# Experts' outputs turned by DMA instead of TensorE, kv's columns permuted, and a new order of tasks

## The chip, the cores and the metric

The kernel runs on one NeuronCore of a Trainium2 chip. The metric is the device time of one execution in microseconds. The kernel before took 221.65 us (median of three runs, 221.53 to 222.14).

## What is computed

There are 8 batches of 576 tokens. A linear attention with 8 heads of 64 feeds a small mixture of 4 attention experts of which each token uses 2:

```
kv  = einsum('bhsd,bhse->bhde', k, v)              # per batch and head: 64 x 64
x   = einsum('bhsd,bhde->bhse', q, kv)
x   = x / sqrt(mean(x*x, -1) + 1e-6) * g_norm      # then heads side by side: (8, 576, 512)
w   = softmax over the best 2 of x @ w_gate        # 4 experts
for e in range(4):
    q, k, v = x @ wq[e], x @ wk[e], x @ wv[e]      # 64 wide
    a  = softmax(causal(q @ k.T / 8))
    out += w[e] * (a @ v @ wo[e])                  # 512 wide
```

## The kernel before

Everything is unrolled. The work is cut into tasks, each a name with a batch and one or two indices; a task is one engine's work on one tile. The string `ORDER` lists all tasks in the order in which they are issued, `ENGINE` says which of DVE (V), ACT (A) and POOL (G) takes each, and `SLOTS` which buffer each tile gets. A planner made the strings offline from costs and due times; each engine, and each DMA queue, works off its own tasks in that order. `ZEROS` puts products on zeros (matmuls that change nothing) ahead of some tasks, so that TensorE stays busy while it waits. SyncE (SP) issues nearly all DMAs in the order of the plan; one that waits holds back those behind it.

Tokens come in five blocks, four of 128 and one of 64. For each batch:

- `lk`, `lv`, `lq` load k, v and q (lines 309, 314, 321, 345); batches 0 and 1 (`NINE`) use another layout, and their q is turned by TensorE, while the later batches' q is turned on DVE (line 476).
- `kv` forms kv on TensorE; `kvc` copies it (line 283, where all copies out of PSUM are recorded) into `kvx`, which also holds, per head, four columns that make the gate's logits; `kgm` and `kgr` (lines 448, 455) compute these columns.
- `out` multiplies q by `kvx`. `oc` copies the result to `o_sb`; `sq`, `red`, `ln`, `rs` and `na` to `nc` make rstd; `xm` (line 562) multiplies x by rstd and sorts the 512 columns into four groups of every fourth column; `x` turns the groups on TensorE and `xc` copies them to `xT`.
- `gl`, `lg` and `m8` to `gate` make the gate's weights.
- `v`, `qp` and `kp` project x. Experts are taken in two pairs. `sc` makes the scores in four pieces, `exp` their exponentials (line 688), `msk` the causal mask (line 694), `pv` the product with v, in two groups of blocks.
- `rc`, `iv` and `oc2` (lines 725, 729, 736) scale the product by the gate over the softmax's sum into `osc`, 128 tokens x 5 blocks x 128 columns in bf16 for a pair.
- `ot` (line 277) turns the five blocks of `osc` on TensorE into PSUM, and `otc` (line 283) copies them to `OT`, of which there are two, for even and odd batches. In the last batch, both are in two parts.
- `y` multiplies `OT` by wo, `yc` copies the result, and `st` (line 779) stores it by SP.

All of TensorE's products are recorded at line 274, its transposes at line 277, all copies at line 283: groups are told apart by their tiles.

In `kvx` a pair of heads lies as four gate columns, 128 columns of kv, four gate columns. rstd's product reads x in order and writes every element to a place 128 elements from the last one:

```
out=short("x", b, i, dtype=FP32R)[:].rearrange("p (c m k r) -> p m k r c", c=NCH, m=NCH, k=2),
in0=ob[:, i, :, E : E + 2 * Dh].rearrange("p m (k r c) -> p m k r c", k=2, c=NCH),
```

Of the kernel before, what the change touches and what calls it, by code (L numbers as in the profile page):

```python
# [23 lines left out]
    ('q', 0, 1): 10, ('kv', 0, 0): 2, ('kv', 0, 1): 3, ('out', 0, 0): 8, ('out', 0, 3): 8,  # L24
    ('q', 1, 1): 8, ('kv', 2, 3): 8, ('out', 1, 4): 6,
# [3 lines left out]
    "04050c0e0100030d020S06070f090A2+0T0U0V320B0Y0I0a0Z0C0b0W0X0g0E2z2-0k5F310h5H0w0x0o0l080m0p305G0s0n0M0y0z1I0q1J"  # L29
    "130r181K333C34140i0G5L0j0t0u19150D165U0v7i1D0+1L0-1E5I0K5M1A1M1b1B1F3E353A101G361C1c3D3B387h5K1H1711371V3F393W"  # L30
    "5T3G5JAC127f3O1d7p0H5O1P1N7g1Q0J1Y3H1Z3P1O3I1S1R1a0N5S1T1W5R5P1U5W3X5V3K3J1X5N3S5Q3Q1e3L3TA47n3U5X3R1w1y3M3N0Q"
    "3Y0F1x3V3Z3a3bA6A31z2M2N2K27247j280L3c2L3d1o1q5Y5a1f1u1m1h257q7o2R1p211g1r5Z2U1v7u2S3e3t7s7r1n7t3h1i5d3f222V2O"
    "7w2P5c7vA51+2X3q2T3i1-3r5b3n3k2W5f3u3j7x262Y2Q5e3s5o5k3v5p5l5w5x3o29205q3l1s3m5m3p1j2Z1t1k3g5n5y2a4A4B4C4D1l5g"
    "5s5t5r4e237y5h7+5i3w7k5j2B2A4c7m4f5u5z2c7l0O4E4d2b5v5+5-3x2C2D3z602F612E0R4F422f43AFAHAG2G622g2H2d3y4P2e4Q4m2h"
    "4n4M2i636H687zCT82AI7-AJ2jAKAL4N4J4j6B4p4K4qAB4R6E696I4k6J654G832I48ADAE4O6A6UA944808188644H3+6V8C452JAO894I8A"
    "6K6L844r8D8E6F66490P2n3-6G6N2o6785CU2tCW462q40A7A8AA86CV47Ce6CEu2r6D2u6Y8K8B8LCb8M87AS8NEtCa8G6W6M8HAP6c4L4o6e"
    "6fAM8FCc7273Cd8I6O8J6dEw8O8P6Z6X704S4T6p416q716j8Q8R4g4hCgCiCf4U774X8S2w4V6k4Y4Z788e4WATCZCh4l4iAN6g6h6P2x748b"
    "6S75AR8c6T6l8Y8T8V2k4a6i8hCX8d6mAQAY6nCY2lCjCkCl4bAZAcAd79AkE-7D7ECoAeAl7A7BAa8Z8f8W6Q6a6b6oCm8X8i4s2vEv8gAb4t"
    "F18a4uAgAmAU8sAh4x4v6R8j9SF2HHAfAVCp908tAn6rAW7FAX4yAi9T7C914zAj4w92Ao939Q8U6s9RCt766tAp9d6x6uAq9eAr8k94959AF3"
    "6v9fF66wAs9BF49X9Y6y6zA-4+4-Cn7HAv7G8u7I7J6+59B29D8v5A7L7M5CAyCqF58+CrB5EzExCs7KF06-5D9E2sAwAtAx537NHICuF7CyF8"  # L40
    "547OCzAzE+Cv50B08l51CwF98wEy2yHKC+C-A+FAB18-8xBGBH7P9C96B6CxB7B3B4D4D8D0D5D997D6BqD1Br98FBAuD79ZDADBD2BsBtD3BQ"
    "BRFC7QDC7RBSB8BK8n7TBLDD8mBTDE7ZHJDF7UBdBe9a5E9bBU7aDGBV8y8o99B9BA7W8z9FDH9UFDBBFGHSDIBXBY8p8qDJ7XHVBZHU9V8rBO"
    "FH9HBP5552HM9GB+B-C1C2HTHW9WBCFFFE7cDY7d9IBuBvDMBaHYBW9cHXHZDb9J9KDNDOBbFM9L9MFNFODVDK56FY57FI9NHLHOBxDPDSDLHa"
    "DQFZDRFPBc9hByFJFKHNDWDXBDBMBNC0FaBIBJ9O9PFL9lDTDU9g9i9jFQ9mFRFUHbFV9nFbHRHcFWDs9k5BBEHeDk2pFXDtFSEE9oFTBwEFFc"
    "DZBzFdBf9pBgDaBFEGHfFeFfHPBhBiFgBlDqDlHQDiBmDmBjHdBnFhFmEHBkDrERE1ESDuE2DvDjDc9qHhHgDxFjFsD+9rFiHiFvDyDdFnDnDg"
    "BoBpD-HjDoDzETFpC3HmDpDhHyHnHoFoEOEIHzC5E3Hk9zEJFyDe9+EPC9HpF-FkFlC4FtFqFr9wFwFzC6H+DfFuC7EL9xCACBHqC8Hu7YHlEQ"
    "GAFxE07VH-HvEMHrF+HsDwG6CCGBCDGgGhHwE4E6HtG7HxI09sI1E7E8EKGeI2GGE5CECKGfGEI3I4GH9yE9GoEAI5IGCLCF7bGFEBCQGpA0A1"
    "CMGOGPGlCRG0I6GiGjI7ECI8G1IDG4IH9tI9IEED9uCS7SGmIMCNIAIBG5ENIJIIIFCOGRGSINGTGI2mGJGLEUG2EVEZIKCH9-GKGqICG8EWGM"
    "CIILIeIOEXCGGCGk9vG3EYEaEbG9IgIhEcIPIaIfGDGrIbGsIo587eCJIpEdGtIQGnIlImIiIUEnGvIVGNGuGQGwEoIcGxGyIjIdJ4J5GUGzGV"
    "J6J7GZGWEhG+IWEiA2EpIRG-GXGaCPInEjH0H1GbGYGcIqIkJHJIIrIsISIXJ8EqItGdHEHFHGJ9JAITJEJFJGErJBJCEsJJHBIYH5H6HCHDEk"  # L50
    "IZEeIuElEmJDJKEfIwIxJMJLH8H9IvIyJPJNJ0JOH7JQJRJ1JSH2JTJUEgIzH3JcHAJdH4I+JZI-J2JVJWJ3JeJaJbJfJgJiJXJYJjJhJk"
)
ENGINE = (
    "VVVVVVVVVVVVVVVGVGVVVGVVVVVAVVVAVVVVVAVVVAVAAVVAAVVVAVVAAVVVAVAAVGVAAVGVAAVGVAAVGVAAVVVVVVVAGVAGVAVVVGVVVGAVGV"
    "VGVVVAVAVAVAVAVVVAGVAGVAGVAGVVVVVVGVVAVAVAVAGVAGVAGVAGVVVVVVVVVVVVVVAVVAVVAVVVVVVVVVVVVAGVVVVAVAVAVAAVVAGVVVGV"
    "VAAVVVAVAAVVVVVVVAGVAGVVGVVGVVVGAVVVVVVAVAVVVVVAVAVAVAGVAGVAGVAGVVVVVVGVVVVAVAVAGVAGVAGVAGVVVGVVGVVVVVVVVVVAVV"
    "AVVAVVVVVVVVVVVVVVVVVVVVVVVVVVVVVAAVVVGVVAAVVVAVVVGVAAVGVGVGVAGVVGVAGVAGVAVGAVGVVGVVVVVAVAVAVVVAVAGVAGVAGVAGVV"
    "VGVVGVVAVVVAVAGVAGVAGVAGVVVGVVGVVAVAVVAVVVVVVVVVVVVVVVVVVVVVVVVVVVVAGVGVVVVVVVGVVAGVVAAVVAGVVAAVAAVGVGVGVAGVAG"
    "VAGVVGVVVVAVGVVVVVVVVAVVVAVAVVVAGVAGVAGVAGVVVVVVGVVAVAVAVAGVAGVAGVAGVVVGVVGVVAVVVVVVVAVVAVVVVVVVVVVVVVVVVVVVVV"
    "VVGVGVVVVVVAAVVVAVVAAVVAGVVVAVAAVGVGVGVAGVVGVAGVAGVAVGAVGVVVVAVVVVVAVAVVVAVAGVAGVAGVAGVVVGVVGVVVVAVVVAGVAGVAGV"  # L60
    "AGVVVVVVVVVAVVVVAVVAVVVVVVVVVVVVVVVVVVVVVVVVVAGVVVVVVVVAGVVVAVVVGVVAAVVAGVAAVGVGVGVVGVAGVVGVAGVVVGAVGVVGVAVVVA"
    "VAVAVAVAVAGVAGVAGVAGVVVGVVGVVVVAVAVAGVAGVAGVAGVVVVVVVVVVVAVVAVVVVVAVVVVVVVVVVVVVVVVVVVVVVVVVVVVVVVVAAVVVAVVAAV"
    "VAGVVVGVAAVGVGVGVVGVVGVAGVVVVVVGAVGVVGVAVAVVVAVVVVVAVAGVAGVAGVAGVVVVVVVVVVVAVVVAGVAGVAGVAGVVVGVVGVVAVAVVAVVAVV"
    "VVVVVVVVVVVVVVVVVVVVVVVAGVGVVVVVVAGVVAAVVAAVVVGVVVAVAAVGVGVGVVGVAVVAGVAGVVVGAVGVVGVVVVVVVAVVVVVAVAGVAGVAGVAGVV"
    "VVVVGVVAVAVVVAVAGVAGVAGVAGVVVGVVVVVVVVVVVVVVVAVVAVVVV"
)
SLOTS = (
    "00112326041501223046172011523620072123130483261500194A1513120B071320123854530148730301456A97021670211103018430"
    "0C101001113200B90313A27015145013140465547232417C5057143081103102202003043A2B3090013132B03328101456610207126020"
    "3201510322138321300103C3419160030321036744856721032210024835427032032005439A3143022400321202320923613302673043"  # L70
    "11620617201201761030201721506127456C013202303452303C120236200131452310C250450301165476723C4A521031004672261117"
    "00213045102413202167420320323112203264074190C10520617450091454427C1"
# [7 lines left out]
def names(nb):  # L80
# [3 lines left out]
    for b in range(nb):  # L84
# [7 lines left out]
        out += [("kvc", b, g) for g in range(1 + (b == 0))] + [(m, b, n) for n in r2 for m in ("kgm", "kgr")]  # L92
# [9 lines left out]
        for p in r2:  # L102
            out += [(m, b, p) for m in ("qp", "qpc", "kp", "kpc")]
            out += [(m, b, p, j) for j in r4 for m in ("sc", "exp", "msk")]
            out += [("pv", b, p, g) for g in r2] + [(m, b, p, g) for g in r2 for m in ("rc", "iv", "oc2")]
            out += [(m, b, p) + t for t in (((),) if b < nb - 1 else ((0,), (1,))) for m in ("ot", "otc")]
# [14 lines left out]
def kernel(  # L121
# [70 lines left out]
    ob = const.tile([P, NB, NCH, 2 * GW], FP32, name="o_sb")  # L192
# [18 lines left out]
    for j in range(2):  # L211
        kvx.append(const.tile([P, EP, 2 * GW], FP32, name=f"kvx{j}"))
        rstds.append(const.tile([P, NB * H], FP32, name=f"rstd{j}"))
        roots.append(const.tile([P, NB * H], FP32, name=f"root{j}"))
        t = const.tile([P, NB, H], FP32, name=f"ms{j}")
        nc.vector.memset(t[REM:P, NB - 1], 1.0)
        mss.append(t)
# [12 lines left out]
    for j in range(2):  # L230
        t = const.tile([P, NCH * S + PAD], FP32R, name=f"xT{j}")
        nc.vector.tensor_copy(out=t[:, NCH * S :], in_=zeros[:, 0:PAD])
        xTs.append(t)
        OTs.append(const.tile([P, EP * S], BF16, name=f"OT{j}"))
# [32 lines left out]

    def gates_of(t):
        return t[:].rearrange("p m (k g) -> p m k g", g=E)[:, :, :: 2 * GW // E - 1, :]
# [100 lines left out]
    def wg(m):  # L370
        rd_(nc.vector.tensor_tensor(
            out=wg_t[:, :, 2 * m : 2 * m + 2, :],
            in0=bank(m, "gb").rearrange("p (c d e) -> p e c d", c=2, e=E),
            in1=g_wide[:].unsqueeze(1).unsqueeze(2).to_broadcast([P, E, 2, Dh]), op=AluOpType.mult,
        ))
# [25 lines left out]
    def p_kv(b, n):  # L401
        if b in NINE:
            return big("kv", b, n if b == 0 else 0)[:, :, 0 : EP * Dh].rearrange("p a (m d) -> p m a d", m=EP)
# [34 lines left out]
    def of_part(b, g):  # L438
        return slice(g, g + 1) if b == 0 else slice(0, EP)

    def kv_copy(b, g):
        ms = of_part(b, g)
        copy(
            ("kvc", b, g), kvx[b % 2][:, ms, E : E + 2 * Dh].rearrange("p m (a d) -> p m a d", a=2), p_kv(b, g)[:, ms]
        )

    def kvg_mul(b, m):
        ew(("kgm", b, m)).tensor_tensor(
            out=short("g", b, m)[:].rearrange("p (e f) -> p e f", e=E),
            in0=kvx[b % 2][:, m, E : E + 2 * Dh].unsqueeze(1).to_broadcast([P, E, 2 * Dh]),  # L450
            in1=wg_t[:].rearrange("p e (m k) d -> p e m (k d)", k=2)[:, :, m], op=AluOpType.mult,
        )

    def kvg_sum(b, m):
        nc.vector.tensor_reduce(
            gates_of(kvx[b % 2])[:, m], tiles["t", "g", b, m][:].rearrange("p (e k d) -> p k e d", e=E, k=2),
# [450 lines left out]
```

## Time and profile before

| | |
|---|---|
| median of three runs | 221.65 us |
| profiled execution: time, span | 220.71 us, 219.0 us |
| mean granted TensorE clock | 0.961 |
| PE / weight loads (PEld) busy | 201.9 / 168.7 us |
| DVE / ACT / POOL busy | 151.6 / 137.5 / 111.2 us |
| moved by DMA | 40.42 MB |
| transposes at line 277 | 80, of 128 x 128 bf16 |
| products on zeros | 53, all before 44 us |

The profile is of one execution. "Busy" is the time in which an engine worked on at least one instruction. The chain of work is followed back from the last instruction to what released it, so that an engine which the chain names for long stretches sets the time there. The granted clock is TensorE's, as a share of full speed. "To landing" is the time from a DMA's issue to its completion.

### The profile page before, as it was taken

What the parts mean: (1) busy time and instruction counts of PE and PEld (TensorE: products, weight loads), DVE (VectorE), ACT (ScalarE), POOL (GpSimd) and SP (SyncE); (2) the same over time, 40 slices, a digit from 0 to 9 for tenths busy, and PEclk for the clock granted to TensorE, in tenths of its full rate; (3) what the DMA queues carried; (4) which work ended last, traced back from release to release, by engine and by line L of the source; (5) the groups of instructions that cost most, each with busy time, mean ns of one, the idle gap of its engine ahead of it and who ended that gap; (6) DMA issues with size and microseconds to landing.
All of it is one profiled execution on the core that took longest, in us unless ns stands there. A gap on an engine that the chain in (4) does not pass through costs nothing.

```text
span 219.0 us, 8779 instructions
## 1 busy us (share of the span) xinstructions
PE 201.9 (92%) x3697; PEld 168.7 (77%) x3697; DVE 151.6 (69%) x392; ACT 137.5 (63%) x253; POOL 111.2 (51%) x215
## 2 busy tenths in 40 slices
PE   6399849798999999999999999999999999999981
PEld 2367546597989988797899799687997897889650
DVE  2017463885896798577788779895987977657662
ACT  2012362344895769948886566877769957954951
POOL 7000003813496697729825953559759528624400
PEclk9676988999999999999999999999999999999996
DMA  5999997696999799979899984992001021922277
GB/s 199 396 380 374 331 293 134 105 236 181 164 298 195 134 291 180 177 189 293 122 181 236 257 133 88 223 200 76 3 3 49 3 99 49 317 91 100 85 265 253
DMA packets 86279, 40.42 MB, mean 185 GB/s; under 512 B 63952, under 2 KB 78816, under 8 KB 86240
## 3 DMA queue, kind: packets, MB, share of 16 engines
q1 hardware_dynamic: 85600, 38.68, 71.7%
q10 hardware_dynamic: 544, 1.18, 1.5%
q8 instruction: 29, 0.48, 1.1%
q14 instruction: 10, 0.08, 0.2%
q0 software_dynamic: 96, 0.01, 0.0%
HBM read 30.42 MB, written 9.44 MB: 182 GB/s over the span
## 4 chain that ended last, share of the span: by engine, by line
PE 87%; DMA 4%; issue 4%; POOL 2%; ACT 1%; DVE 1%; SPq 0%; POOLq 0%
PE p L274 84%; DMA kvq<-in_q_dram 4%; PE p L277 2%; POOL tmp L562 1%; ACT PT L688 1%; POOL PT L694 1%; DVE o_sb L283 0%; ACT tmp L283 0%; SPq L309 0%; DVE tmp L283 0%; ACT OT L283 0%; POOL inv L729 0%; POOL g_gt L608 0%; POOLq L562 0%
## 5 line engine op out<-in xcount | busy, mean ns | idle before, releaser
L688 ACT ACTIVATE PT<-p 128x1024 bf16<-128x1024 f32 (+1 forms) x64 | 51.7, 839 | 8.7 <-PE p L274 7.2
L562 POOL TENSOR_TENSOR tmp<-o_sb,rstd 128x512 fp32r<-128x512 f32 x35 | 37.9, 1116 | 4.7 <-PE p L274 3.1
L694 POOL TENSOR_SCALAR_AFFINE_SELECT PT<-PT 128x256 bf16<-128x256 bf16 (+1 forms) x80 | 30.0, 399 | 12.0 <-ACT PT L688 12.0
L510 DVE TENSOR_REDUCE ms<-sq 128x8 f32<-128x520 f32 (+1 forms) x40 | 26.7, 682 | 6.8 <-ACT sq L504 3.4
L274 PE MATMUL p<-kvq,kvq 64*64 64x64 f32 (+1 forms) x768 | 25.1, 242 | 2.9 <-issue 2.9
L274 PE MATMUL p<-kvx,kvq 64*64 64x68 f32 x1152 | 25.2, 223 | 2.2 <-issue 1.9
L506 POOL TENSOR_TENSOR sq<-o_sb 128x512 f32<-128x512 f32 (+1 forms) x15 | 15.5, 1037 | 22.7 <-ACT o_sb L283 11.5
L274 PEld LDWEIGHTS p<-kvq,kvq 64*64 64x64 f32 (+1 forms) x768 | 22.4, 154 | 5.7 <-issue 3.9
L274 PEld LDWEIGHTS p<-kvx,kvq 64*64 64x64 f32 x1152 | 21.7, 133 | 6.4 <-issue 3.8
L274 PE MATMUL p<-wv_r,xT 128*128 128x256 f32 x160 | 26.4, 297 | 0.0
L274 PE MATMUL p<-ident_r,tmp 128*128 128x128 f32 (+1 forms) x160 | 23.8, 282 | 0.0
L534 POOL TENSOR_TENSOR root<-root,ms 128x40 f32<-128x40 f32 (+1 forms) x10 | 2.7, 273 | 40.4 <-DVE root L528 40.4
L274 PEld LDWEIGHTS p<-wv_r,xT 128*128 128x128 f32 x160 | 21.2, 189 | 2.0 <-issue 0.9
L274 PE MATMUL p<-qTp,kT 64*128 64x64 f32 (+4 forms) x192 | 22.5, 341 | 0.0
L274 PEld LDWEIGHTS p<-ident_r,tmp 128*128 128x128 f32 x160 | 20.6, 191 | 2.1 <-issue 0.4
L274 PE MATMUL p<-wo_b,OT 128*128 128x512 bf16 (+1 forms) x96 | 21.0, 348 | 0.4 <-ACT OT L283 0.4
L274 PE MATMUL p<-xT,wq_r 128*128 128x288 f32 x128 | 20.1, 299 | 0.0
L283 ACT COPY o_sb<-p 128x544 f32<-128x544 f32 (+1 forms) x24 | 14.1, 617 | 9.1 <-PE p L274 5.9
L274 PE MATMUL p<-xT,wk_r 128*128 128x288 f32 x128 | 19.8, 299 | 0.0
L283 DVE COPY o_sb<-p 128x544 f32<-128x544 f32 (+1 forms) x16 | 11.4, 718 | 10.5 <-PE p L274 6.7
L504 ACT ACTIVATE sq<-o_sb 128x512 f32<-128x512 f32 (+1 forms) x25 | 15.8, 632 | 4.3 <-DVE ms L510 2.4
L274 PE MATMUL p<-vext,PT 128*128 128x65 bf16 x480 | 18.1, 193 | 0.0
(96 smaller groups left out, 347.2 us busy)
## 6 DMA issues: line engine op xcount, KB each, us to landing
out_dram<-tmp SPq DMA_DIRECT2D x32, 256.0 KB, 2.9
kvq<-in_q_dram SPq DMA_DIRECT2D x48, 144.0 KB, 5.7
kvq<-in_k_dram SPq DMA_DIRECT2D x6, 1024.0 KB, 9.0
kvq<-in_v_dram SPq DMA_DIRECT2D x6, 1024.0 KB, 7.5
kvq<-in_q_dram SPq DMA_DIRECT2D x4, 576.0 KB, 10.6
kvq<-in_k_dram SPq DMA_DIRECT2D x4, 576.0 KB, 10.3
kvq<-in_v_dram ACTq DMA_DIRECT2D x2, 576.0 KB, 7.1
kvq<-in_v_dram SPq DMA_DIRECT2D x2, 576.0 KB, 10.1
```

The source lines that it names most:

```text
L274: done.append(nc.tensor.matmul(*args, **kwargs))
L277: done.append(nc.tensor.transpose(*args))
L283: rd_(nc.scalar.copy(dst, src) if engine[task] == "A" else nc.vector.tensor_copy(out=dst, in_=src))
L504: nc.scalar.activation(dst, src, ACTF.Square)
L506: nc.gpsimd.tensor_tensor(out=dst, in0=src, in1=src, op=AluOpType.mult)
L510: nc.vector.tensor_reduce(mss[b % 2][:nt, i, :], sqs[(NB * b + i) % 3][:nt], axis=AX_X, op=AluOpType.add)
L534: ew(("nb", b, g)).tensor_tensor(out=roots[b % 2][:, cols], in0=roots[b % 2][:, cols], in1=ms[:, cols], op=AluOpType.mult)
L562: ew(("xm", b, i)).tensor_tensor(out=short("x", b, i, dtype=FP32R)[:].rearrange("p (c m k r) -> p m k r c", c=NCH, m=NCH, k=2), in0=ob[:, ...
L688: rd_(nc.scalar.activation(PT[:, :, d0 : d0 + o], big("sc", b, pr, j)[:, :, 0:o], ACTF.Exp, scale=scale))
L694: nc.gpsimd.affine_select(out=d, in_=d, compare_op=AluOpType.is_ge, fill=0.0, base=0, pattern=[[0, 2], [1, w]], channel_multiplier=-1,)
```

## The change

1. For batches 0 to 6 the tasks `ot` and `otc` give way to one task `dt` for each pair of experts, a DMA issued by SP that reads `osc` (128 x 640 bf16) and writes its five 128 x 128 blocks, turned, to `OT`. Batch 7 keeps `ot` and `otc` in two parts. `OT` gets room for five whole blocks.
2. The copy of kv permutes the 64 columns of each head, so that every fourth column comes to lie beside the next; g_norm's product with w_gate (`wg`) is permuted to match, in two instructions where there was one. Each head in `kvx` and `o_sb` has its four gate columns first, then 64 columns. rstd's product then reads and writes runs of 16.
3. In batch 1 kv is copied in two parts, with a PSUM tile each, as in batch 0.
4. `ORDER`, `ENGINE`, `SLOTS` and `ZEROS` are new. There are 82 products on zeros instead of 53, again all ahead of work of batches 0 to 2. Of the 40 rstd products, 14 are on DVE (5 before) and 26 on POOL (35); of the squares, 20 on POOL (15) and 20 on ACT (25).

The plan's strings are left out here:

```diff
 ZEROS = {
-    ('q', 0, 1): 10, ('kv', 0, 0): 2, ('kv', 0, 1): 3, ('out', 0, 0): 8, ('out', 0, 3): 8,
-    ('q', 1, 1): 8, ('kv', 2, 3): 8, ('out', 1, 4): 6,
+    ('gg',): 16, ('kv', 0, 0): 2, ('q', 0, 0): 7, ('out', 0, 3): 13, ('kv', 1, 0): 13,
+    ('kv', 1, 1): 10, ('kv', 2, 3): 10, ('out', 1, 2): 7, ('out', 1, 1): 4,
 }
...
-            out += [(m, b, p) + t for t in (((),) if b < nb - 1 else ((0,), (1,))) for m in ("ot", "otc")]
+            out += [("dt", b, p)] if b < nb - 1 else [(m, b, p, g) for g in r2 for m in ("ot", "otc")]
...
-        kvx.append(const.tile([P, EP, 2 * GW], FP32, name=f"kvx{j}"))
+        kvx.append(const.tile([P, NCH, GW], FP32, name=f"kvx{j}"))
...
-        OTs.append(const.tile([P, EP * S], BF16, name=f"OT{j}"))
+        OTs.append(const.tile([P, EP, NB * P], BF16, name=f"OT{j}"))
...
     def wg(m):
-        rd_(nc.vector.tensor_tensor(
-            out=wg_t[:, :, 2 * m : 2 * m + 2, :],
-            in0=bank(m, "gb").rearrange("p (c d e) -> p e c d", c=2, e=E),
-            in1=g_wide[:].unsqueeze(1).unsqueeze(2).to_broadcast([P, E, 2, Dh]), op=AluOpType.mult,
-        ))
+        src, by = bank(m, "gb").rearrange("p (h r c e) -> h p e c r", h=2, c=NCH, e=E), g_wide[:].rearrange("p (r c) -> p c r", c=NCH)
+        for h in range(2):
+            rd_(nc.vector.tensor_tensor(
+                out=wg_t[:, :, 2 * m + h, :].rearrange("p e (c r) -> p e c r", c=NCH),
+                in0=src[h], in1=by.unsqueeze(1).to_broadcast([P, E, NCH, Dh // NCH]), op=AluOpType.mult,
+            ))
...
     def kv_copy(b, g):
-        ms = of_part(b, g)
-        copy(
-            ("kvc", b, g), kvx[b % 2][:, ms, E : E + 2 * Dh].rearrange("p m (a d) -> p m a d", a=2), p_kv(b, g)[:, ms]
-        )
+        t, dst = p_kv(b, g), kvx[b % 2][:, :, E:]
+        if b in NINE:
+            t, dst = t[:, g], dst[:, 2 * g : 2 * g + 2]
+        else:
+            t = t.rearrange("p m a d -> p (m a) d")
+        copy(("kvc", b, g), dst.rearrange("p h (c r) -> p h c r", c=NCH), t.rearrange("p h (r c) -> p h c r", c=NCH))
...
-            out=short("x", b, i, dtype=FP32R)[:].rearrange("p (c m k r) -> p m k r c", c=NCH, m=NCH, k=2),
-            in0=ob[:, i, :, E : E + 2 * Dh].rearrange("p m (k r c) -> p m k r c", k=2, c=NCH),
...
+            out=short("x", b, i, dtype=FP32R)[:].rearrange("p (c h r) -> p h c r", c=NCH, h=H),
+            in0=ob[:, i, :, E:].rearrange("p h (c r) -> p h c r", c=NCH),
...
+    def turn_by_dma(b, pr):
+        nc.sync.dma_start_transpose(
+            OTs[b % 2][:, pr].rearrange("p (n t) -> p n t", n=NB), tiles["osc", b, pr][:].rearrange("p n e f -> p (n e f)")
+        )
+
...
-            lhs = OTs[b % 2][:, pr * S + s0 : pr * S + s0 + nq]
+            lhs = OTs[b % 2][:, pr, s0 : s0 + nq]
```

## The prediction

> **What bounds the kernel now.** I read the head of the profile page first, then the chain of work that ended last in order of time, then busy time by stage. The page says that TensorE (PE) is busy for most of the span and that the chain runs over it:
>
> ```profile
> PE 201.9 (92%) x3697; PEld 168.7 (77%) x3697; DVE 151.6 (69%) x392; ACT 137.5 (63%) x253; POOL 111.2 (51%) x215
> PE 87%; DMA 4%; issue 4%; POOL 2%; ACT 1%; DVE 1%; SPq 0%; POOLq 0%
> ```
>
> The table by stage (length, then busy time of PE, PEld, DVE, ACT, POOL, then granted clock, DMA share, GB/s) shows where this holds:
>
> ```profile
> 0.00:51.50 51.50, 40.45 (x984) 28.58 (x985) 25.65 (x64) 15.20 (x31) 12.50 (x30) 0.87 0.92 262
> 51.50:79.80 28.30, 28.30 (x525) 26.22 (x525) 21.77 (x54) 21.09 (x42) 19.41 (x30) 1.00 0.97 220
> 79.80:150.00 70.20, 69.85 (x1262) 60.63 (x1262) 55.40 (x142) 53.62 (x96) 44.26 (x80) 1.00 0.96 192
> 150.00:208.50 58.50, 58.29 (x870) 50.62 (x871) 44.26 (x120) 44.41 (x79) 34.62 (x75) 1.00 0.22 76
> ```
>
> From 51.5 us to 208.5 us PE is busy 156.4 of 157.0 us at full clock: whatever PE no longer does there comes off the end, as long as nothing new makes it wait. Before 51.5 us it is idle for 11 us, and the clock is at 0.87. DMA is nearly full until 150 us and mostly free after it.
>
> **What is removed.** In the chain, one pair's five transposes (L277) are a piece by themselves:
>
> ```profile
> 79.78 0.39 PE p L277 x5
> 80.17 3.52 PE p L274 x51
> 83.69 0.39 PE p L277 x5
> ...
> 176.60 0.29 PE p L277 x5
> 176.90 8.27 PE p L274 x88
> ```
>
> Batches 0 to 6 have 14 such pairs. Their pieces, 0.28 to 0.39 us each (two of them are the one piece of ten, 0.57 us), add up to 4.56 us. All lie in the full stage, so **-4.56 us** if PE never waits for the replacement. The 14 evacuations of the transposed outputs (L283 into OT: 7 on DVE at 454 ns, 7 on ACT at 639 ns, 7.7 us in all) go too; both engines have over 20% idle time in these stages, so I count nothing. Batch 7 keeps its transposes: the tail after 208.5 us, with its store, is as before.
>
> **What is added: 14 transposing DMAs on SP's queue.** No row of this trace shows such a transfer. It moves 128 x 640 bf16, 160 KB. What counts is the time L from its issue to its landing against the PE work that the new plan puts between the moment the pair is scaled (L736) and the first product with OT that needs it. I read both out of the plan's strings and give each task its rows' time (8 matmuls of q's or k's projection 1.25 us, 4 of v's 0.66, a 128-token y 0.57, score pieces 0.25 to 0.68, a P.V group 0.45 or 0.68). Rows overlap (all PE rows sum to 243.5 us, busy is 201.9), so I multiply by 0.83, and take off 0.5 us for the scaling itself. For batch 6: y 0.57, three score pieces 0.68 + 0.62 + 0.45, v 0.66, y 0.57, v 0.66, y 0.57, scores 0.25, y 0.36 make 5.4, times 0.83 is 4.5, less 0.5 is 4.0 us. In the same way batch 5 has 5.1, batches 4 and 3 7.0, batch 2 7.1, batch 1 7.4 and batch 0 9.3 us. These are **the covers**.
>
> L is bounded by the nearest rows. These are of stores, also issued by SP and also with SBUF as source, first after 150 us, then from 60 to 130 us, and of loads of q in small runs from 60 to 130 us:
>
> ```profile
> out_dram<-tmp SPq DMA_DIRECT2D x17, 256.0 KB, 3.0
> out_dram<-tmp SPq DMA_DIRECT2D x10, 64.0 KB, 2.1
> ```
> ```profile
> kvq<-in_q_dram SPq DMA_DIRECT2D x29, 144.0 KB, 6.2
> ...
> out_dram<-tmp SPq DMA_DIRECT2D x2, 256.0 KB, 4.2
> ```
>
> Low end 2.1 us; high end 9.1 us, the longest q load. I take the store's rows, nearest in size, source and queue: 3.0 us for batches 3 to 6, which have quiet queues, 4.2 us for batches 0 to 2. Every cover is longer, so **0**. At 6.2 us batches 6 and 5 lose 2.2 + 1.1 = 3.3 us; at 9.1 us all but batch 0 lose, 5.1 + 4.0 + 2.1 + 2.1 + 2.0 + 1.7 = 17.0 us.
>
> A rule of the Trainium skill speaks against this change. "VectorE: DVE Perf Modes", section "The three transpose paths", gives 390 ns on TensorE and 1309 ns through the DMA crossbar for one 128 x 128 bf16 block, and its rules send such a block to TensorE where PSUM will do. This trace has 219 ns for one TensorE transpose and 56 to 78 ns in a row of five; no run here shows the other. If five blocks went one after the other, 6.5 us plus the 2.1 us floor would be an L of 8.6 us, by my estimate from that page, and the covers would lose 14 us: slower by 9. "Advanced Engine Details and Errata", section "X-Bar Transpose (TRN2)", says instead that such transfers are as fast as regular ones; then the covers hold.
>
> On SP, a waiting transpose holds what is queued behind it: for batches 0 to 2 loads of batches 5 to 7, for 3 to 6 stores. Issuing is not free either: a q load's issue holds SP 0.8 us in the median, up to 4.2, in a stage in which SP issues almost without a pause. Six transposes at 0.5 to 4.2 us are 3 to 25 us of SP, 5 at the median; their 0.96 MB at that stage's 210 GB/s are 4.6 us of DMA. The cover: the last q load is issued at 143.2 and lands within 6 us, the transposes on DVE (L476) that read it begin from 157.9 us. 9 us cover 5, so 0; without cover up to 5 us at the median, and more at the far end. A transpose into OT must also wait until the batch two before has read OT; the plan puts it behind those reads.
>
> **kv's columns.** rstd's product (L562) wrote single elements 512 bytes apart and will write runs of 16. The row of the weights' scaling (L384) is a product of that size with runs: 668 to 798 ns on DVE against 1103, 1033 to 1040 ns on POOL against 1116:
>
> ```profile
> L562 DVE TENSOR_TENSOR tmp<-o_sb,rstd 128x512 fp32r<-128x512 f32 x5 | 5.5, 1103 | 0.0
> L384 DVE TENSOR_TENSOR wk_r<-tmp,g_rows 128x512 fp32r<-128x512 f32 x1 | 0.7, 668 | 0.0
> ```
>
> The plan moves nine of them from POOL to DVE: DVE 14 x 0.7 - 5 x 1.1 = +4.3 us, POOL 26 x 1.04 - 37.9 = -10.9 us. PE's full stage hides either: 0. The copy of kv (376 ns for 256 columns on ACT) now reads PSUM with a step of four. It could cost nothing, as the copies of turned q do, which also permute (1.23 ns an element against 1.13 for a plain one), or as much more as the product did (1.6 times); only the four copies of batches 0 and 1 lie ahead of an idle PE: 0 to 1.0 us, 0.1 taken. wg_t's product in four halves adds about 0.3 us on DVE ahead of a product that waits for kv anyway: 0.
>
> **The new plan's beginning.** The same products stand before the first scores of batch 0, but the plan issues 82 matmuls on zeros where there were 53. In the trace rows of them take 1.90 us for 8 to 3.62 us for 10, 0.24 to 0.36 us each: 29 more are 7.0 to 10.4 us. PE idles 9.8 us ahead of 51.5 us (1.4, 2.7, 0.6, 2.9, 1.1 and 1.0), so all could fall into idle time. Beyond that, the clock loses 0.13 x 51.5 = 6.7 us, and a PE kept busier may get some back. Bounds +10 and -6.7; I take 0, since the zeros are put ahead of tasks that wait for loads, as before.
>
> **Sum.** -4.56 + 0.1 is -4.5 us; with 0.2 for a late transpose here or there, -4.3. The profiled execution took 220.7 us (span 219.0), so 216.4. The three runs' median is 221.65, 0.9 above it; carried over, **217.4 us**. About 0.3% is what a measurement of this kernel can tell: faster is below 221.0, slower above 222.3.
>
> **The rivals.**
> A, the forecast: covers hold, the beginning costs what it did. 217.4, from 216 to 219. For it: PE full for 157 us, covers above the store's row. 0.45.
> B, the beginning pays: about ten of the added zero matmuls stand in PE's way, 10 x 0.3 = 3 us: 220.4, from 219 to 222.5. For it: 29 more against 9.8 us of idle time leaves little over; against it, idle time moves with the loads. 0.17.
> C, the transposes land late. The place is the first y of batches 6 and 5, where PE, in order, stands still for L less 4.0 and 5.1 us. The sum reaches the 4.5 us gained at an L of 6.8 us; above that it is slower than before. At 8 us: 4.0 + 2.9 + 1.0 + 1.0 + 0.9 + 0.6 = 10.4, so 227.6 (the 0.2 us above is part of it); at 9.1 us 234. For it: no row shows the transfer, and q's loads, with small runs, need 6.2 us where the queues are full; against it, after 150 us they are empty. 0.28, most of it slower.
> D, the beginning gains: half of the clock's 6.7 us comes back: 214.0. 0.10.
> That the product doesn't get shorter in runs would cost 9 x 0.4 us on DVE, which has idle time in every stage: no time of its own.
>
> Faster: A, D and 0.11 of B, 0.02 of C, 0.68. Within 0.3%: 0.03 of B and of C, 0.06. Slower: 0.26. The range runs from D to C at 8 us, 214.0 to 227.6, and leaves out the later part of C and a still better beginning.
>
> **What would show it.** L277 down to 10 instructions; the transposes' issue-to-landing at or under 4 us in the list of DMA issues; no wait of PE or PEld on a DMA into OT after 80 us; L562 near 0.7 us on DVE; PE's full stage shorter by 4 to 5 us and its start still near 51 us. It is wrong if PE waits for OT, or if SP's queue holds the loads until kv of batch 6 or 7 is late.

## The result and the profile after

The changed kernel took 229.35 us (median of four runs, 227.6 to 230.6) against 221.59 us for the kernel before: a ratio of 1.034 with a 95% interval of 1.027 to 1.042. It is slower by some 7.8 us; the forecast was 4.3 us faster. In the profiled execution the span is 228.3 us (219.0 before). A kernel's executions fall into a faster and a slower state, and a ratio compares those in the faster one alone, so that it can differ from the ratio of the medians.

The head of the page after, busy time of PE and the others and then the chain of waits by engine:

```profile
PE 199.5 (87%) x3656; PEld 164.4 (72%) x3656; DVE 157.5 (69%) x404; ACT 128.4 (56%) x241; POOL 106.8 (47%) x204
PE 69%; DMA 12%; issue 5%; SPq 4%; DVE 4%; ACT 2%; POOL 2%; DVEq 0%
```

PE does a little less than before (201.9 us) and the span is 9.3 us longer, so PE waits more. The chain says on what: DMA's share went from 4% to 12%, the share of SP's queue from 0 to 4%. The table by stage of the kernel after, in the stages of the prediction, shows where:

```profile
0.00:51.50 51.50, 38.53 (x990) 26.76 (x990) 21.64 (x55) 10.67 (x26) 19.56 (x37) 1.00 0.94 258
51.50:79.80 28.30, 25.00 (x429) 21.75 (x430) 22.02 (x48) 18.25 (x35) 13.45 (x22) 0.94 0.93 189
79.80:150.00 70.20, 64.37 (x1164) 57.19 (x1163) 56.64 (x140) 45.99 (x88) 36.66 (x65) 1.00 0.96 185
150.00:208.50 58.50, 58.50 (x939) 50.42 (x939) 47.83 (x134) 43.63 (x79) 33.10 (x68) 1.00 0.38 107
```

Where PE had been full from 51.5 us on, it is now full only from 150 us on; it loses 3.3 us of busy time in the second stage and 5.5 us in the third. In the second stage these are two waits, 0.6 us ahead of a product with wv and 2.7 us ahead of kv of batch 3; in the third, 3.3 us for a load of v and 2.4 us in two waits for copies by DVE. The loss ends where DMA's share falls from 0.96 to 0.38.

The clearest account goes by four points that each kernel passes: PE's first product for kv of batch 4, that of batch 7, PE's last instruction, and the end of the span. The last two columns are two runs told of below.

| us | before | after | after, run again | before without its transposes |
|---|---|---|---|---|
| start to kv of batch 4 | 77.4 | 84.0 | 85.8 | 76.8 |
| to kv of batch 7 | 64.5 | 68.0 | 64.8 | 64.1 |
| to PE's last instruction | 72.7 | 70.0 | 70.1 | 69.8 |
| to the end of the span | 4.4 | 6.3 | 6.8 | 4.3 |
| span | 219.0 | 228.3 | 227.5 | 215.0 |

Two of these points stand in PE's timeline, that of before first, then that of after (start, length, product):

```profile
77.36 1.62 PE L274 MATMUL p<-kvq,kvq 128*64 128x64 f32 x48
```
```profile
84.01 2.08 PE L271 MATMUL p<-kvq,kvq 128*64 128x64 f32 x64
```

The first transposing DMA is issued at 85.6 us. So 6.6 of the 9.3 us were lost **before any transposing DMA ran** (8.4 of 8.5 in the second run). In the run shown all of it was lost even before kv of batch 3, which PE begins at 64.3 us (60.4 before): from there to kv of batch 4 PE has no pause in either kernel, and what it takes longer there (19.7 us against 16.9) is work that the old plan had done ahead of kv of batch 3, 378 products against 357. Up to kv of batch 4 both have issued about as many, zeros left out (1400 and 1397). Behind kv of batch 7 the new kernel gains 2.7 us: there the removed transposes show. At the end it loses 1.9 us again.

And the new transfers are as quick as forecast. The row of the 14 transposes by tile, and what landed when (issue on SP in ns, landing in us, each least, median, longest), in the kernel after:

```profile
L736 SPq DMA_TRANSPOSE OT<-osc x14: 1200/1350/2798, 85.6 to 210.6; - x14
DMA to landing us min/median/max: 2.6/2.8/4.5
```

No wait of PE or of PEld on a DMA into `OT` is in the kernel after. What the chain shows instead are loads of weights, k and v (start, length, what), here the two longest pieces that are a DMA after the first microseconds:

```profile
45.33 5.88 DMA tmp<-in_moe_wv_dram
...
96.72 11.89 DMA kvq<-in_v_dram
```

The first is the half of wv that comes last. SP issues it 10.5 us later than before, and k of batch 3 12.8 us later. SP's timeline, before and then after:

```profile
34.81 0.61 SPq L378 DMA_DIRECT2D tmp<-in_moe_wv_dram  x1
...
41.84 0.94 SPq L314 DMA_DIRECT2D kvq<-in_k_dram  x1
```
```profile
45.33 0.40 SPq L376 DMA_DIRECT2D tmp<-in_moe_wv_dram  x1
...
54.62 1.94 SPq L311 DMA_DIRECT2D kvq<-in_k_dram  x1
```

This half of wv lands at 51.2 us, k of batch 3 at 64.2, 9.6 us after its issue. Here are PE's products that need them, in the kernel after (in brackets the idle time ahead and what ended it):

```profile
52.08 1.14 PE L271 MATMUL p<-wv_r,xT 128*128 128x256 f32 x4 [1.46 <-DVE wv_r L382]
...
64.30 2.09 PE L271 MATMUL p<-kvq,kvq 128*64 128x64 f32 x64 [2.72 <-ACT PT L680]
```

The new plan loads wv later and also uses it sooner: PE's first product with it came at 57.3 us before. For the second wait the profile names the exponentials of the scores, of which the last ended at 63.96 us; k of batch 3 landed behind them. In the run with six loads later, told of below, kv of batch 3 begins 1.5 us behind the first scores instead of 3.6.

The second piece is v of batch 5: PE was ready for it at 105.4 us and stood 3.3 us. In SP's queue this load stands behind the first two transposing DMAs, which held SP from 85.6 to 90.4 us, so a part of this wait may be theirs. In the second run of the same kernel there is no such wait.

Other loads come only just in time. Before, from 55 us on (the 1 MB load of v is batch 4's):

```profile
55.93 2.22 SPq L314 DMA_DIRECT2D kvq<-in_v_dram  x1
```

After, where the last line is the same load:

```profile
56.60 7.47 SPq L342 DMA_DIRECT2D kvq<-in_q_dram  x3
64.17 1.27 SPq L318 DMA_DIRECT2D kvq<-in_k_dram  x2
65.47 2.25 SPq L342 DMA_DIRECT2D kvq<-in_q_dram  x2
...
72.02 2.35 SPq L342 DMA_DIRECT2D kvq<-in_q_dram  x2
74.41 3.96 SPq L311 DMA_DIRECT2D kvq<-in_v_dram  x1
```

SP issues v of batch 4 18.5 us later than it did, with pieces of q ahead of it. It lands 9.5 us after its issue, at 83.9 us, and PE comes to kv of batch 4 at 84.0 without a pause. By the plan's strings, the number of q's loads, of a batch or a later one, that stand ahead of the later one of the batch's big loads of k and v went from 2, 1, 0, 0, 0 (batches 3 to 7) to 4, 4, 5, 5, 5. The new plan also uses q sooner: DVE first turns q of batch 4 25 tasks behind the batch's first kv product (111 before), that of batch 3 53 tasks behind (133 before).

### The profile page after: what moved, and what is told of

Its sections match the earlier page's. It is cut to its first block, busy times and chain, and to the rows that moved or that the text cites. A ratio compares the mean times of both kernels' runs of the same rounds, so it can differ in the third digit from the quotient of the medians.

```text
span 228.3 us, 8679 instructions
## 1 busy us (share of the span) xinstructions
PE 199.5 (87%) x3656; PEld 164.4 (72%) x3656; DVE 157.5 (69%) x404; ACT 128.4 (56%) x241; POOL 106.8 (47%) x204
## 3 DMA queue, kind: packets, MB, share of 16 engines
q1 hardware_dynamic: 95008, 40.97, 76.8%
## 4 chain that ended last, share of the span: by engine, by line
PE 69%; DMA 12%; issue 5%; SPq 4%; DVE 4%; ACT 2%; POOL 2%; DVEq 0%
PE p L271 69%; DMA kvq<-in_v_dram 5%; DMA kvq<-in_k_dram 5%; DMA tmp<-in_moe_wv_dram 3%; SPq L318 2%; SPq L342 1%; POOL sq L501 1%; DVE o_sb L280 1%; ACT PT L680 1%; DVE g_mk L594 1%; SPq L306 1%; DVE ms L505 1%; POOL tmp L445 1%; ACT o_sb L280 1%; SPq L376 1%
## 5 line engine op out<-in xcount | busy, mean ns | idle before, releaser
L505 DVE TENSOR_REDUCE ms<-sq 128x8 f32<-128x520 f32 (+1 forms) x40 | 26.8, 679 | 10.2 <-POOL sq L501 8.6
L501 POOL TENSOR_TENSOR sq<-o_sb 128x512 f32<-128x512 f32 (+1 forms) x20 | 20.7, 1038 | 26.2 <-ACT o_sb L280 16.2
L555 POOL TENSOR_TENSOR tmp<-o_sb,rstd 128x512 fp32r<-128x512 f32 x26 | 28.9, 1131 | 7.6 <-DVE rstd L536 6.4
L271 PE MATMUL p<-kvq,kvq 64*64 64x64 f32 (+1 forms) x768 | 22.7, 223 | 7.3 <-DMA kvq<-in_v_dram 3.3
L271 PE MATMUL p<-wv_r,xT 128*128 128x256 f32 x160 | 27.6, 302 | 1.5 <-DVE wv_r L382 1.5
L271 PEld LDWEIGHTS p<-kvq,kvq 64*64 64x64 f32 (+1 forms) x768 | 20.1, 136 | 10.9 <-issue 7.0
L271 PE MATMUL p<-zeros 128*128 128x512 bf16 (+1 forms) x82 | 18.4, 369 | 7.9 <-issue 6.2
L271 PE MATMUL p<-ident_r,tmp 128*128 128x128 f32 (+1 forms) x160 | 22.6, 279 | 0.0
L271 PEld LDWEIGHTS p<-xT,wq_r 128*128 128x128 f32 x128 | 17.7, 188 | 2.1 <-ACT qTp L280 1.6
L271 PEld LDWEIGHTS <-zeros 128*128 128x128 bf16 x82 | 7.8, 105 | 15.9 <-issue 10.2
L280 ACT COPY o_sb<-p 128x544 f32<-128x544 f32 (+1 forms) x22 | 13.2, 619 | 10.6 <-PE p L271 10.6
L473 DVE STREAM_TRANSPOSE kvq<-kvq 128x576 f32<-128x576 f32 x24 | 18.0, 758 | 1.5 <-DMA kvq<-in_q_dram 1.4
## 6 DMA issues: line engine op xcount, KB each, us to landing
kvq<-in_v_dram SPq DMA_DIRECT2D x2, 576.0 KB, 10.3
```

Of the source, the lines that this page charges most:

```text
L271: done.append(nc.tensor.matmul(*args, **kwargs))
L280: rd_(nc.scalar.copy(dst, src) if engine[task] == "A" else nc.vector.tensor_copy(out=dst, in_=src))
L473: nc.vector.transpose(t[:, i * S : (i + 1) * S], tiles["L", "q", b][:, i * S : (i + 1) * S])
L501: nc.gpsimd.tensor_tensor(out=dst, in0=src, in1=src, op=AluOpType.mult)
L505: nc.vector.tensor_reduce(mss[b % 2][:nt, i, :], sqs[(NB * b + i) % 3][:nt], axis=AX_X, op=AluOpType.add)
L555: ew(("xm", b, i)).tensor_tensor(out=short("x", b, i, dtype=FP32R)[:].rearrange("p (c h r) -> p h c r", c=NCH, h=H), in0=ob[:, i, :, E:].r ...
```

## The experiments

Theory: the new plan's order of loads costs the time, the transposing DMA little. Rival: the transposing DMA itself (its traffic, its issue, or SP held while it waits) costs it. Each run's ratio is to the kernel before on the same chip; that took 222.3 to 223.0 us.

### The plan without the transposes, and the transposes without the plan

**The new plan without any transposing DMA.** It leaves out the transposes of batches 0 to 6; `OT` holds a constant.

```diff
+    for t in OTs:
+        nc.gpsimd.memset(t[:], 0.5)
...
+            if n[0] == "dt":
+                continue
```

> The changed kernel with the transposing DMAs of batches 0 to 6 left out: OT is filled once with a constant and y of these batches multiplies that, so the transposes cost nothing at all and hold nothing up. Theory P (the plan's beginning and its loads): it stays at or above 224 us, within 4 us of the changed kernel. Theory Q (the transposes hold SP's loads and land late): it falls to 217 to 221 us, 8 us or more below the changed kernel.

Measured: 226.72 us, 1.019 [1.014, 1.024].

**The kernel after, run again beside it**, unchanged.

> The changed kernel, unchanged, on the chip of the next three: 3 to 5% above the kernel before. It is what the next is read against.

Measured: 228.74 us, 1.030 [1.024, 1.035]. The transposing DMAs are worth 0.011 of 222.5 us in the new plan, 2.4 us.

**The old plan without transposes.** The same for the kernel before: no transposes and no copies of them for batches 0 to 6.

```diff
+            if n[0] in ("ot", "otc") and n[1] < B - 1:
+                if n[0] == "ot":
+                    place(("sm",) + n)
+                continue
```

> The kernel before with the transposes of batches 0 to 6 and their copies left out (OT filled once with a constant, y multiplies that): what the removal alone is worth in the old plan. By the prediction's first term 4.6 us below the kernel before, 217 us; if PE's time there is not what sets the end, less than 2 us.

Measured: 219.57 us, 0.979 [0.971, 0.986]. So the removal is worth 2.9 us by the medians, 4.8 by the ratio, and the new plan is slower than the old one by 7 us by the medians and by 1.019 / 0.979 = 1.041, some 9 us, by the ratios, **with no transposes in either**. The plan lost the time. Whether it was the order of its loads this pair does not tell: PE's order, the engines, the buffers and the zeros differ too.

**The permuted columns alone**, in the kernel before, with its old plan (here rstd's product; the other lines are those of the change):

```diff
-            out=short("x", b, i, dtype=FP32R)[:].rearrange("p (c m k r) -> p m k r c", c=NCH, m=NCH, k=2),
+            out=short("x", b, i, dtype=FP32R)[:].rearrange("p (c h r) -> p h c r", c=NCH, h=H),
```

> The kernel before with the other part alone: kv's columns permuted in its copy, g_norm's product with w_gate permuted, rstd's product in runs of 16 (batch 1's kv is copied in two instructions by the same engine). Plan as before, transposes on TensorE. Theories P and Q: no change, 221 to 222 us, since rstd's product is off the chain; the product on DVE falls from 1103 to about 700 ns. A rival that the permuted copy of kv is dear: 223 us or more.

Measured: 222.4 us, 0.997 [0.991, 1.003]: no change. Its rows of the product (mean ns behind the comma):

```profile
L558 POOL TENSOR_TENSOR tmp<-o_sb,rstd 128x512 fp32r<-128x512 f32 x35 | 36.1, 1043 | 4.7 <-PE p L271 3.1 <-DVE rstd L539 1.4 <-DVE inv L724 0.2
L558 DVE TENSOR_TENSOR tmp<-o_sb,rstd 128x512 fp32r<-128x512 f32 x5 | 4.2, 839 | 0.0
```

It got shorter by 7% on POOL (1116 before) and by 24% on DVE (1103).

**The transposing DMA in the old plan**, first right behind the scaling (`ot` and `otc` are left out as above). In this kernel a DMA can write `OT` ahead of the y of two batches before, so that y uses a later batch's values:

```diff
+            if by_dma and n[0] == "oc2" and (n[0], n[1], n[2], 1 - n[3]) in seen:
+                emit["dt"](n[1], n[2])
```

> The kernel before with one part of the change: in batches 0 to 6 the pair's five transposes and their copy give way to the transposing DMA on SP, issued right after the pair's second scaling; plan, data layout of kv and zeros stay. Theory P (the new plan's beginning and its order of loads cost the time; the DMA itself pays): 217 to 219 us, 3 to 4.5 below before. Theory Q (a waiting transposing DMA at SP holds loads behind it, wherever it stands in the stage of loads): 223 to 227 us, with waits of PE on loads between 80 and 150 us. Theory R (the transposing DMAs land too late for y): PE waits for OT, above 225 us; the 2.8 us to landing in the changed kernel speak against it.

Measured: 242.89 us, 1.079 [1.065, 1.094]. Then with each DMA behind the scaling and behind the last y of two batches before:

```diff
+                if scaled and all(b < 2 or ("y", b - 2, i) in seen for i in range(NB)):
+                    turns.remove((b, pr))
+                    emit["dt"](b, pr)
```

> The kernel before with the transposing DMAs on SP in the place of the transposes, each right after the pair's second scaling, or after the last y of two batches before where that is later. Theory P: within 2 us of the kernel before without any transposes. Theory Q: 8 us or more above that, with PE waiting for loads or for OT between 80 and 150 us.

Measured: 237.99 us, 1.072 [1.066, 1.078], some 20 us slower than the old plan without transposes (18 by the medians). The longest waits of SP in it (engine, line, releaser; us, times, longest):

```profile
SPq L744 <- DVE osc L736: 22.5, 7, 10.9
SPq L744 <- DVE xT L283: 11.1, 1, 11.1
SPq L744 <- PE p L274: 7.9, 4, 3.9
```

SP runs ahead of the other engines with its loads. A transpose in its queue pins it to the place where `osc` gets ready: these three rows are 41.5 us in which loads and stores queued behind it were not issued. Here the DMA also came too late for its reader, by PE's waits (us, times, longest):

```profile
PE p L274 <- DMA OT<-osc: 10.3, 2, 6.4
```

The same DMA costs 2.4 us in the plan that was made with it. SP stands nearly as long there (32.1 us in its two longest rows, shown further below), but its two longest pauses, 8.3 and 9.0 us, come after 156 us, when all loads have been issued. So the transposing DMA is cheap only where the plan leaves SP room, and it was not the main cause of the loss.

**The same for batches 3 to 6 only**, where DMA is mostly free (the edit against the kernel of 237.99 us):

```diff
-            if n[0] in ("ot", "otc") and n[1] < B - 1:
+            if n[0] in ("ot", "otc") and 3 <= n[1] < B - 1:
```

> The kernel before with the transposing DMA in batches 3 to 6 alone, where few loads are left; batches 0 to 2 keep their transposes on TensorE. Theory Q (the harm is done by holding back loads and by full queues): at or below the kernel before, 0.985 to 1.00. If the harm comes from the DMA in whatever place (SP holds stores, y waits): above 1.02.

Measured: 232.77 us, 1.031 [1.022, 1.041]. SP still stood 34.6 us at the transposes for `osc`, up to 13.2 us at a time; loads of q of batch 7 that had been issued at 137 to 144 us came from 153 us on. Free DMA engines did not help a queue that was held.

**The same for all of them, but later in SP's order**, at most 25 tasks ahead of the batch's first y (again against the kernel of 237.99 us):

```diff
-                if scaled and all(
+                if scaled and at[n] >= at["y", b] - 25 and all(
```

> Before, with the transposing DMA for batches 0 to 6 and no transposes or copies for them, each DMA now put into SP's order at most 25 tasks ahead of the batch's first y (the kernel that put it right behind the scaling took 1.072). Theory (what cost there was SP held by a DMA that waits for osc, with loads behind it): SP's waits at the transposes fall from 47.8 us to under 25, and the time to 1.01 to 1.045. Rival (the DMA's own traffic costs, or PE's waits for OT): it stays at 1.06 to 1.08, or PE's waits for OT grow from 10 us to over 15.

Measured: 248.24 us, 1.114 [1.102, 1.126]: worse, and neither side's forecast. SP's wait for `osc` stayed at 22.9 us. The reading "move it later and SP waits less" falls.

**The traffic and the issue alone:** the old plan without its own transposes, with 14 transposing DMAs that turn a constant tile into a spare one, so that none waits for `osc` and nobody waits for one. The expert outputs of batches 0 to 6 are a constant's.

```diff
+                    nc.sync.dma_start_transpose(spare[:], OTs[b % 2][:, 0 : NB * P])
```

There is one spare tile, so a transpose waits until the one before it has landed.

> Before without its transposes and copies of batches 0 to 6, and with the same 14 transposing DMAs at the places of the kernel that took 1.072, but turning a constant tile into a spare one, so that none waits for osc and nobody waits for one: the traffic and the issue alone (the outputs of these batches are not the reference's; without any such DMA the kernel took 0.979). Theory (SP held at the wait for osc is what cost 16 to 18 us): 0.98 to 1.00 of before. Rival (the traffic or the issue of the transposes itself): 1.03 to 1.07.

Measured: 226.72 us, 1.023 [1.017, 1.028], between the two forecasts: 0.044 or 10 us above the run without them (7 by the medians). So up to half of the 20 us is there without any wait for `osc`. Not all of that is traffic and issue: SP stood at four of the transposes for the one before, which only the single spare tile asks for (us, times, longest):

```profile
SPq L889 <- DMA spare<-OT: 8.1, 4, 4.5
```

What SP's delays do shows in the timeline of DVE in this run:

```profile
145.75 0.69 DVE L285 COPY tmp<-p 128x512 f32<-128x512 f32 x1 [2.82 <-DMA out_dram<-tmp]
...
153.97 0.42 DVE L285 COPY tmp<-p 128x256 f32<-128x256 f32 x1 [5.10 <-DMA out_dram<-tmp]
```

These are copies of y. They wait for a buffer whose store stood in SP's queue behind transposes and loads. What stands behind the copy on DVE waits too, and so does PE from 151.4 us on, for 3.2 us. Then comes a second price, in the table by stretch (PE's busy time, then its granted clock):

```profile
150.00:156.00 6.00, 2.85 (x45) 0.86 0.95 198
156.00:162.00 6.00, 6.00 (x95) 0.57 1.26 204
```

**Transposes by ACT's queue in the new plan**, to take them off SP:

```diff
-        nc.sync.dma_start_transpose(
+        nc.scalar.dma_start_transpose(
```

> The changed kernel with the transposing DMAs issued by ACT's queue instead of SP's: they hold no loads, but ACT waits for the scaling and spends the issue, 14 times 1.35 us. Theory Q: 223 to 227 us, kv of batch 5 begins some 4 us earlier than at 108.75 us. Theory P: within 2 us of 229.4.

Measured: 241.46 us; its four times ran from 235.66 to 244.31, too far apart for an interval, all above the kernel after. In its profiled execution, of 243.4 us, SP's loads waited for the other queue's transposes:

```profile
SPq L342 <- DMA OT<-osc: 9.1, 2, 5.8
SPq L311 <- DMA OT<-osc: 7.9, 1, 7.9
SPq L318 <- DMA OT<-osc: 6.8, 1, 6.8
```

**Transposes on TensorE in the new plan**, at the places of the DMAs, with the copies on ACT or DVE:

```diff
+            if n[0] == "dt":
+                turn_on_pe(*n[1:])
+                continue
```

> The changed kernel with the transposes put back on TensorE, each pair's five and their copy at the place of the transposing DMA in the plan, in a PSUM bank that is free there. Theory P: the plan stays slow and the transposes come back on PE, 231 to 234 us. Theory Q: SP is free of waits, the loads of batches 5 to 7 come earlier, 222 to 227 us.

Measured: 245.77 us, 1.103 [1.094, 1.111]. It is no fair undoing. A place that suits SP is none for PE, ACT and DVE: PE stood 7.6 us ahead of its transposes, and ACT and DVE stood 24.8 us, in 14 waits, for the transposes that they copy. It says nothing on the loss.

### What in the plan costs the time

Theory: the order of loads. Rivals: the 29 added zero products; PE's order itself.

**Six loads later** (four pieces of q of batches 3 and 4, both halves of wo), behind k of batch 3:

```diff
+    LATER = (("lq", 3, 1), ("lq", 3, 5), ("lq", 3, 2), ("lq", 4, 3), ("lwo", "o", 0), ("lwo", "o", 1))
```

> The changed kernel with six loads that nothing needs for another 20 us or more (q of batch 3 in three parts, q of batch 4 in one, both halves of wo) issued after k of batch 3 instead of ahead of the last weights. If the new order of loads makes the beginning late (the product with wv waits until 52 us, kv of batch 3 until 64 us), both come 2 to 4 us earlier and the time falls to 1.01 to 1.02 of the kernel before, from 1.03. If the beginning is late for another reason (zeros, engines), it stays at 1.03.

Measured: 230.42 us, without an interval (its times ran from 226.8 to 232.9); no gain. The first scores came at 57.1 us instead of 61.7, kv of batch 3 at 58.7 instead of 65.0, both as expected. But kv of batch 4 stayed at 85.3. In between, DVE and then PE, in this run:

```profile
70.24 0.78 DVE L473 STREAM_TRANSPOSE kvq<-kvq 128x576 f32<-128x576 f32 x1 [5.81 <-DMA kvq<-in_q_dram]
```
```profile
72.68 2.26 PE L271 MATMUL p<-xT,wk_r 128*128 128x288 f32 x8 [4.22 <-DVE g_den L605]
```

Now q of batch 3 was late, and DVE stood for it.

**Fewer zeros:** without the 44 of the 82 that stand ahead of kv of batches 1 and 2 and of products of batch 1.

```diff
-    ('gg',): 16, ('kv', 0, 0): 2, ('q', 0, 0): 7, ('out', 0, 3): 13, ('kv', 1, 0): 13,
-    ('kv', 1, 1): 10, ('kv', 2, 3): 10, ('out', 1, 2): 7, ('out', 1, 1): 4,
+    ('gg',): 16, ('kv', 0, 0): 2, ('q', 0, 0): 7, ('out', 0, 3): 13,
```

> The changed kernel without the 44 products on zeros that stand ahead of kv of batches 1 and 2 and of out of batch 1 (38 of 82 are left). If they stand in PE's way: 2 to 5 us less, 1.01 to 1.02 of the kernel before. If they fill waits for loads: no change, or up to 3 us more by a lower clock.

Measured: 229.42 us, 1.021 [1.015, 1.027]. Against the kernel after (1.030 [1.024, 1.035] on another chip) that may be 1% less; the intervals overlap.

**Both edits:**

> Both: the six loads later and 44 zeros fewer. If loads and zeros are each part of the cost, below either alone, 0.99 to 1.01 of the kernel before.

Measured: 228.11 us, 1.024 [1.018, 1.029]. The two together give no more than the zeros alone.

**q behind k and v throughout:** from batch 3 on, a piece of q is loaded only when k and v of its batch have been issued, and wo behind k of batch 3.

```diff
+            wait_for = [("lk", 3, 0)] if n[0] == "lwo" else [("lk", n[1], 0), ("lv", n[1], 0)] if n[0] == "lq" and n[1] >= 3 else []
+            if not set(wait_for) <= seen:
...
+                later.append((n, set(wait_for)))
+                continue
```

> After, with one rule on top of its plan: from batch 3 on, a piece of q is loaded only when SP has issued the big loads of k and v of its own batch, and the two halves of wo only behind batch 3's k; all else in its order. Theory (the new plan lost its time to the order of its loads): kv of batch 4 starts at 77 to 81 us instead of 85.8, kv of batch 5 at 98 to 104 instead of 107.2, kv of batch 7 at 143 to 147 instead of 150.6, and the time is 1.00 to 1.015 of before, 223 to 226 us. Rival (PE's own new order and its zeros carry the loss, and the late loads only fill time that would be lost in any case): kv of batch 4 comes 2 us earlier at most and the time stays at 1.02 to 1.035. A third way (q then comes late): PE stands at q's copies of batch 4 or 6, and the time is over 1.03.

Measured: 235.42 us, 1.058 [1.048, 1.068], slower still. kv of batch 4 came at 80.5 us, 5.3 us earlier, as the theory wanted. Then the third way happened. SP, DVE and PE in this run:

```profile
71.90 13.33 SPq L342 DMA_DIRECT2D kvq<-in_q_dram  x8
```
```profile
87.25 0.78 DVE L473 STREAM_TRANSPOSE kvq<-kvq 128x576 f32<-128x576 f32 x1 [3.90 <-DMA kvq<-in_q_dram]
```
```profile
88.49 1.08 PE L271 MATMUL p<-ident_r,tmp 128*128 128x128 f32 x8 [3.06 <-DVE vext L280]
```

And in the table by stretch, PE's busy time and granted clock:

```profile
84.00:90.00 6.00, 2.94 (x40) 1.00 0.79 127
90.00:99.00 9.00, 9.00 (x107) 0.50 0.96 260
99.00:102.00 3.00, 3.00 (x32) 0.80 0.50 44
```

A pause of 3 us was followed by 9 us at a granted clock of 0.50, which cost another 4.5 us (9 x 0.5, an estimate).

**The same with fewer zeros:**

> The kernel with q behind k and v, and besides without the 44 zero products that stand ahead of kv of batches 1 and 2 and of y of batch 1 (38 stay). Theory (both belong to the beginning, and add up): 2 us below the kernel with the loads alone, 0.995 to 1.01 of before. Rival (the zeros only fill waits): within 0.5% of the kernel with the loads alone.

Measured: 237.66 us, without an interval (235.4 to 241.1): nothing gained.

**q's loads made cheap, in both plans** (of the edit, the lines of the source are shown). Each load of q from batch 2 on reads one contiguous block: as many bytes in runs of 4.6 KB instead of 128 bytes. q's values are wrong by it.

```diff
-            q[b, h0 : h0 + 2, :, (r % 2) * 32 : (r % 2 + 1) * 32].rearrange("h (g t) d -> t (h g) d", t=32),
+            q[b, h0 + i % 2].rearrange("s d -> (s d)").rearrange("(p x) -> p x", p=32),
```

> After, with every load of q from batch 2 on reading one contiguous block of q (as many bytes, but 4.6 KB at a time instead of 128 bytes; q's values are wrong by it, the instructions behind are the same). Theory (the new plan lacks transfers, not work: it wants q of batch 4 beside k and v of batch 4 while the DMA engines are full): kv of batch 4 starts at 76 to 80 us instead of 85.8 and the time falls by 6 to 10 us, to 0.98 to 1.00 of before. Rival (PE's own order and zeros cost it): it falls by 0 to 3 us and stays over 1.015.

> Before, with the same edit of q's loads. Theory: the old plan has its transfers in time, so it gains 0 to 3 us (0.985 to 1.00 of before), and the distance between the two plans falls from 7 us to under 2.5 us. Rival: both plans gain alike, and the distance stays at 5 to 8 us.

Measured: after with it 230.04 us, 1.029 [1.020, 1.038]; before with it 224.43 us, 1.009 [1.001, 1.017]. In the new plan kv of batch 3 came at 62.0 us instead of 65.0 and kv of batch 4 at 81.5 instead of 85.8, but the time did not fall (1.030 without the edit): that is the rival's forecast, by which PE's own order and the zeros cost it. The distance between the plans is 2.0% instead of 3.0% only because the old one got slower; by the medians it is 5.6 us. So it is not shown that slow transfers of q cost the new plan its time. The edit was also weaker than meant: the share of the SP loads' and stores' queue in the DMA engines' time fell only from 77% to 67%, and a 1 MB load of k took 10.2 us to land instead of 7.5.

## Why the prediction was wrong, step by step

- **"-4.56 us" for the transposes: about right.** Taking them out of the old plan gave 2.9 us by the medians, 4.8 by the ratio, and the last full stage of the new kernel is 2.7 us shorter. L277's 80 transposes are 10 now, as foreseen.
- **L and the covers: right.** 2.8 us in the median, 2.6 to 4.5, against 3.0 and 4.2 taken. In the kernel after, PE never waits for a DMA into OT. The prediction's estimate from the Trainium skill's "VectorE: DVE Perf Modes", section "The three transpose paths", an L of 8.6 us for five blocks one after the other, does not fit here: the five blocks land in 2.8 us. What one block takes alone no run here shows. "Advanced Engine Details and Errata", section "X-Bar Transpose (TRN2)" (as fast as regular transfers), agrees: a store of 256 KB takes 2.6 us in the same profile. Rival C did not come true in the new plan; in the old one PE did wait for OT, 10.3 us.
- **SP's hold, "9 us cover 5, so 0": wrong in kind, small here.** It priced the issue of six transposes, against a cover for the loads' landing. It named the hold by a waiting transpose, but put no time to it: how long SP stands until `osc` is there. In the kernel after the longest of these waits are

```profile
SPq L736 <- DVE osc L728: 19.5, 6, 9.0
SPq L736 <- PE p L271: 12.6, 7, 6.9
```

  Whether that costs is the plan's doing: 2.4 us in the new one, some 20 us in the old one, PE's waits for OT among them.
- **The permutation, "0.1 taken": right in the old plan** (0.997 [0.991, 1.003]). The product is shorter on DVE (860 ns in the kernel after, 1103 before), but not by as much as the 0.7 us used; on POOL, 1131 ns there, it is not shorter. What the nine products more on DVE cost in the new plan was not tried by itself.
- **"The new plan's beginning ... I take 0": the step that failed.** It weighed 29 zeros against the idle time of PE and against the clock, and took for granted that "the same products stand before the first scores" means the same time. The products are nearly the same. The data is not there: first scores at 60.7 us against 56.8, kv of batch 4 6.6 us late, before the first transposing DMA. The old and the new plan without transposes differ by 7 to 9 us. The zeros took less than the sum had (82 are busy for 18.4 us, the 53 were for 14.3), and leaving 44 of them out gave perhaps 2 us (not shown beyond the intervals). That loads are late at the beginning is shown, by PE's waits for wv and for k of batch 3 and by each load that was moved: what was hastened came earlier by 4 to 6 us. But no reordering paid. What had been put behind was then late, and DVE or PE stood for that: the new plan wants k, v and q of a batch almost together (25 tasks between kv and q's turn in batch 4, where there were 111), while the DMA engines' share is 0.93 to 0.96 until 150 us. That this is the whole of the 7 to 9 us is not shown. Every forecast of a shorter time by better loads failed, and cheaper q loads brought kv of batch 4 forward by 2.5 to 4.3 us and left the time as it was. How much PE's own order, the engines and the buffers of the new plan cost stays open.
- **"The tail after 208.5 us, with its store, is as before": wrong by 1.9 us.** From PE's last instruction to the end it is 6.3 us instead of 4.4, and 6.8 in the second run. DVE's last copies of y come 1.1 us behind PE's end there, after 2.4 us of idle time of DVE; why is not shown:

```profile
223.09 1.02 DVE L280 COPY tmp<-p 128x512 f32<-128x512 f32 x2 [2.37 <-issue]
```

- **The rivals.** B had the right place and the wrong mechanism and size: 3 us for zeros that stand in the way. The clock that D hoped for came (1.00 before 51.5 us, where it had been 0.87) and the kernel was slower all the same. No rival let the order of the loads decide, though both plans' strings and the 0.97 of DMA's share in the second stage were there to read.
- **"PE busy 156.4 of 157.0 us ... whatever PE no longer does there comes off the end, as long as nothing new makes it wait":** the condition was the point. Something new did make it wait: in the new plan PE was full only where its loads came in time.

No version tried here that does the whole work beats the kernel before.

## What to carry to other kernels

When a change brings a new order of work, price the order first: go through the loads in the order of their queue and compare, for each, the place of its issue with the place of its first use, in both plans; in a stage in which DMA's share was 0.93 to 0.96, as here, a load that was moved ahead made another one late. A DMA that waits for a computed tile does not belong in the one queue that also runs ahead with the loads, unless the loads behind it are not needed soon and the stores behind it don't hold a buffer that an engine waits for. And an engine that is full in the profile may be full only because its loads land just before they are needed, as v of batch 4 did here; how much room they have shows in the time between landing and use, not in the engine's busy time.

## What the runs showed of the hardware that was not expected

- A transposing DMA of 160 KB lands in 2.6 to 4.5 us, like a store; its issue holds SP for 1.2 to 2.8 us, 1.35 in the median, and 1.2 to 2.0 where it waits for nothing that is computed.
- Transposes issued by ACT made loads issued by SP wait for them (23.8 us in three rows of that run). Whether the chip or the program asks for this wait is not shown.
- After a pause of PE of 3.06 us, the granted clock was 0.50 for the next 9 us of full work in the run with q behind k and v, and after one of 3.15 us it was 0.57 for 6 us in the run with the constant tile. Not always: in the kernel after, PE worked only 0.43 us from 105 to 108 us, and its clock stayed at 1.00 up to 117 us.
